# A linear-attention and Fourier-mixing kernel whose first part's order of steps is written anew

## The chip, the cores and the metric

The kernel runs on one core of a Trainium2 chip. A core has TensorE (PE) for matrix products, VectorE (DVE), ScalarE (ACT) and GpSimd (POOL) for the rest, SyncE (SP), from whose queue nearly all DMAs are issued here, and 16 DMA engines that move data between the device's memory (HBM) and the on-chip buffer (SBUF). TensorE writes only to PSUM, which has eight banks. The metric is the device time of one launch in microseconds (us): the median of several runs. A profile is one more execution, recorded instruction by instruction.

## The reference, cut to what matters

The inputs are q, k, v of shape (8 batches, 8 heads, 576 rows, 64), omega (128 x 64), and two weights, 512 x 2048 and 2048 x 512, given in double precision. In outline:

```python
def phi(x):                              # x is q or k, scaled by 64 ** -0.25
    h = x @ omega.T - sum(x * x) / 2
    return exp(h - max(h)) / sqrt(128)
kv  = phi(k).T @ v;  z = sum(phi(k))     # per batch and head
att = phi(q) @ kv / (phi(q) @ z + 1e-6)
x   = att, heads side by side            # (8, 576, 512)
u   = x + real(fft2(x))                  # over rows and columns of each batch
un  = (u - mean(u)) / sqrt(var(u) + 1e-6)
out = u + relu(un @ w_ch1) @ w_ch2
```

## The kernel before

**Two parts.** The program has a first part, which does attention, the Fourier mixing, the narrowing of the weights from 64 to 32 bits and the first 512 of the 4608 rows of the MLP, and a second part, which does the other 4096 rows in eight blocks of 512 with a scheme of seven products for eight. The second part is the larger, and the change leaves its instructions and their order alone. It begins on TensorE with the first product at line 1359.

**Streams.** The first part is written as generators, called streams, which yield a `Step` (line 103) ahead of each piece of work: the engines that may do it, what it needs to be finished, which buffers and PSUM banks it takes and gives back. The streams, in the order in which they are handed to `listing.run` (line 1319): `first` (omega transposed), `loads` (line 391: k and q of two heads, 288 KB each, into two buffers called `kq`), `loads_v` (line 411: v of two heads, three buffers `vd`), `load_tables` (line 441), `frames`, `plain_norms`, `mixing` (line 766 for each batch), three times `pairs` (each takes every third pair of heads through `attn`), `w2_parts`, `weight_sums`, `block_norms`, `plain` (line 1112: the MLP of the first rows), `weights` (line 480: 32 loads of 512 KB into four buffers `slab`, each followed by `narrow`) and `warm`. A stream can fork others, such as an eviction from PSUM that may wait while the stream goes on.

**One pair of heads** (`attn`, line 611) is: wait for k and q; transpose them by 64-wide matmuls against an identity (line 525) and copy them out (564 on DVE, 566 on ACT); 72 small products with omega (line 644); row maxima on DVE (587); exponentials on ACT (604); 72 small products with v (678); another transpose; products with kv (725 and 733); the division (742 to 754). The mixing of a batch folds its rows and columns by symmetries on DVE and POOL (782 to 823), multiplies with cosine and sine tables on TensorE (844, 854, 894), adds the halves up (943 to 961) and stores the result in HBM (930, 975, 986). `plain` is 512 products of 128 columns (1143) and 128 products of 512 columns (1166). They need nothing of the pairs of heads that are then in work, only rows mixed before and narrowed weights.

**What sets the order.** Each engine runs its instructions in the order in which the program lists them. That order is not found while the program is built: the string `PICKS` (line 65) holds it. `Listing.run` (line 204) keeps a list `todo` of the streams that have a step to do. For each step it reads two characters. The first is a place in `todo`; the second holds, as 9 times the choice of engine plus the PSUM bank, which engine of those that the step allows does the work and in which bank its product goes (8 stands for none; so "h", which is 17, is the second engine with no bank):

```python
pick = next(picks, None)
n = place(pick) if pick else 0
other, self.bank = divmod(place(next(picks)), 9) if pick else (None, None)
...
for item in todo if pick is None else [todo[n]]:
    got = self.start(*item[2:], other=other)
```

A stream whose step is done goes to the end of `todo`. `Listing` also keeps a model of time with the constants of `FIRST` (line 51) and the costs of the steps. Where `PICKS` is read it decides nothing but what it records; it is with such a replay that a string like `PICKS` is searched. As `FIRST` and the steps stand in the kernel, the model knows the loads' time on the DMA engines (270 bytes per ns, one after the other), but nothing of TensorE's instructions having to be fetched.

The instructions of all engines are in HBM, and are brought in while the program runs. The profile lists these transfers as queues of the kind "instruction".

Of the kernel before, what the change touches and what calls it, by code (L numbers as in the profile page):

```python
# [39 lines left out]
class Clock(NamedTuple):  # L40
# [22 lines left out]


PICKS = (
    "4818f8d0f808e3e8d848d4d8d6e20838b8c4f6e8g8a8f8a8f8f8b4ehb8e8e8d4e0dhd8b2d8f8a838e478a8a6bhdh92d8e888b4dhc8b6d8"
    "b4e890ehe2e898h8ghb8j808a4i8i87880i878h488j8ahi8i8g8b8c8h0h88876h2g8i8f0h8e8h8e8g8g8c6fha8e4fh88c0i6i8j8g8i8g8"
    "j8j8g4i8d2j8j898j8a6j8h8dhj8j8f8f8j8i8e0i8f6ih78d2hhbhh8g0hhc8g4g8f8e6h2g8d4i0a8d898h8f898i8c6chj8k8c4j8b8j8h0"
    "i8i8j8j8a6i8i898i8f4i8i818ah78c2i6i8ahb8i4j0i86898dhb8k8k85898k6l4k8k8a2khb8j6i4l0l8i868d8d858g6e2i8f8e8m8m8i8"
    "chn0k8o868h8n8n8ihn8n8n8g4mhl2m8c8m8j8m8k498n868n8h6e2m858d8d6f898i8i878b860e4i6h8h898h8b8c2g88858h8b6i4a8j8j8"  # L70
    "d8b8h8e8i8ghb2h89878b8ch68d8j860l6l8l2d8n8k8j8l8l888i864ghi8b8i8d8j8j888g876j0i8ihg8h4khk6k8i8bhf8k8j8j87078k8"
    "68g898k8j8j8d4k8k886khk0kh68g86hj8j8g8a8h878i6i8g288l8i4d0p6g8m2n8b8l8k88878b8a8h8a6k8j8f0k8k87878h8h8d4j8k8j6"
    "e8fhe0g8k8i8e8j8h2k8l8k4k8j8g8k89h68i8e8d2lh68d0m2m8lh98n8a6e8q8q8q8h8c8m8m0o8n898a8o8b6n8f8b2m8l8m888m8m8g808"
    "h8k87894n098f8l8e6l8j868d8f858b85892g0d6i4f8j8e8g848h8i8jhihg8e8i858a0h8h8b4a8g8e8i8d898i8c8i0i8h8h2i8c0c842jh"
    "b8j8i6h2j8f8gh58i8e0khk4kh48j6k8i8d0m8c2g8n888hhk6n8j8d8e4n8n8a8n8i8i0m8g8h89hm898e8b8c6c8j864i8f88hc8h8j8i8k8"
    "32k3l5khj878j0l1i8ghc8l848f8l8d8i8l6e868l8m8l8i8a8i2n8h8chj8l8l878k874l0m2n6khk858j858l4l8l0f8k898e2b8ehh878a8"
    "i8d858d6h4g8g8d8i898j888hh60khk1l2m3khi8nhb878b8hhb8m898eh96khk2k8k4khb8a8j8i0j8i8h882j6j8k8i8j8j8e8h4h8i8i888"
    "f868f8d0f8f8f858f8f85658f85248f0g8ehc8f8f848b8c1e3d8d8d0dh74d86872dh7hdha0f84876i4h8h8d0i258g848i8f8e6i4g8h8d8"
    "h870k2j8e8k8k8i8j8j8c4i8i8d0i8g6j8e8g4k882k8987hi8i8b8g4kh88k86898d853k2e8m8i8iha8f838k878l8i8c8k84448i848b8g2"
    "h8f858h8h8d8g8a84460k6j8j8h8j888j8j8a2i8i0j8k8k866chk864f8m89858n848kh8880ohj8d2o8h6o8g8m0o2p6n8o868q868j8f8b8"  # L80
    "n8c8n8n8m8d8m8d8o8nhh8h8q8e8a8n8d8n8j8g8d0n2nhk8n8g8h866m8m858l8e8e8fhg878m8c858c0k2k8a878k8b8j856k898k8e888c8"
    "80h298i8i8d8i888a8f8c8d0d8c8f8g8d8f8f8d6f2f8d8c8e8g87858e8a8f86808dhd8dhdha8a8c5e2e846f0g2eh88g8b8c8ch98c82834"
    "c8c8c896c8c852c8c0d4c8d6d8cha0ch88c8c8b298d4dhd6dhb868a0b8c8b2c8d848chc8b4c856e7dhe0dhdh82e688a8e878dhd8d8dh80"
    "dh4898d89488d8d890ch98c898c8c86hb8b8d878d8d8d866d8d7e2f3d8f0f8ehd864e0f266chchd4f8c880e8a2f3989hf8f8f8f868d4f8"
    "dh80fh67f868eh9864c8c87856b8b83880b8b888b4c608bh68c8c8c8c89hb8b852b8483038c2d6d83874e5dh8880e638987hb818834h6h"
    "f8f8f868a8e8f898g8d8chhhh8h8a8a8h8c86660i8i8a8j8e8b8i8i854fhi0j838f8e8f8jhjhe838a8l8l898m8m8m8i8m8b6l8b8k4l8k8"
    "f068m888i8a8h868e8i8j4h8j8j8j8j876k0j8ihkh68h8h6l2l8g8f5h8a8i8m8ihg8k8h4j8j0j8j2ehj5l6g8i8l8g8k8k878k8h8g8g7fh"
    "9892ihf8h4i0d8j8h8gh26i2h860j8g8i8c5h868589hhh50g84hg84888e8a2f3a8g898a0b8b8ah68f8e8e8b8d8dh18b2d8e866f4d898h8"
    "h8dhc8h88842h8a41830i8i8i8f85h7h42hhh5hh6he8h8e8g8g8g8g8gh8890g2g8fh96f89894f890fh98f89hc692f8e4dh68e082g8e8g8"
    "c8f838c6f882g890g8g8b8a2f8687h94g0b898a8g8e6f8h2dhchd8f4f85hdhb0eh46e8g888c4gh90g877ghe0c8g4j6i8k898d3k2l848c8"  # L90
    "l8l8e8k8k8485hih50j6c8j4h8k8k898h8g8j8d8i8f0i8ehf858h896h0ghfhhhh8h8h8h8h8e4i6e8g8h0h8e418i8i8b8f8c8g818a8d8ah"
    "08d8h890b8h4f8h8386876h8f86848a8h828h8h8hhhhd8983h38h8h88876h8a8g4h0g8g8d85888g8f8f80812f8d8c8dh445860f8e88228"
    "b8g886g81888f0f8f4a8g89hdh96eh78d8f8c8b0e432f82878b8e8a8d86888d868d856d8a852d888a6d8e8e8ehc898e8b4e850f8f6ghg2"
    "g8f8g8e8f8ah66gh5872g8e4g886g8b8d2f8a8c0g4g8a878g876b872c8f8a8e4b8g8g8a2h858i8c8c4h8h868g8a8h8c0g8c8g8f4fh76f8"
    "68c0f868a858d86hd868c882ch9476d8d0d878b2c89698a4b8b8b0a888986888a8a8b6c4b8886298b8a8a85898989h8698a8a848448888"
    "42885h8h48609h5894a09h82b6b8948hb08846b8c898b852a878a8869858ah88a850a8a88h88528478468898886844567h70825854965h"
    "5h6888886898429h90989498929888a89ha84098987488467898989898989h6828a8a0a8a1b2c3chc4d5e0589hd1f3g74hehf3b8b8b8f8"
    "fhg8f8089846d878883885489h5h81a6a8884h9834960818a8289828308248380824766855988878989h98a85888888888567h086h4818"
    "98685878686818384858083848083848282838182818081808"
)  # L100


# [1578 lines left out]
```

## Time and profile before

| | |
|---|---|
| time, median of 3 runs | 1172.77 us (1171.44 to 1174.62) |
| the profiled execution | 1177.47 us, of which span 1175.7 |
| granted TensorE clock, mean | 0.992 |
| instruction transfers, q8 | 103 packets, 1.69 MB |
| instruction transfers, q14 | 48 packets, 0.39 MB |
| all other transfers | 218.35 MB |
| TensorE's first product of the second part | at 425 us |

The span is the time from the first to the last instruction of the profiled execution; the rest of its time lies around it. "Busy" is the time in which an engine ran at least one instruction. In lists of instructions the first two numbers are start and duration, and what stands in brackets is the idle time ahead of the instruction and what ended it. A DMA share is the mean busy share of the 16 DMA engines. A loaded stationary operand (PEld) and a matmul are an instruction each.

### The profile page before, as it was taken

The page shows a single profiled execution, that of the slowest core. Times are in us where ns is not written, and L with a number is a line of the kernel's source. Part 1 is how long each engine was busy: PE and PEld are TensorE (multiplying, and loading weights), DVE is VectorE, ACT ScalarE, POOL GpSimd, SP SyncE. Part 2 cuts the span into 40 slices and gives each one's busy share as a digit, 9 for nine tenths or more (in the row PEclk, how much of TensorE's full clock was granted, in tenths as well). Part 3 has the DMA queues.
Part 4 walks back from the last instruction along what each step waited for, and adds up shares of the span by engine and source line. Part 5 has one row for each costly group of instructions (what it writes and reads, how often), then busy time and mean ns, then how long its engine had stood idle before and what let it go on. Part 6 is the DMA issues. An engine that isn't in the chain of part 4 may idle for free.

```text
span 1175.7 us, 32543 instructions
## 1 busy us (share of the span) xinstructions
PE 1139.7 (97%) x13045; PEld 1019.1 (87%) x13045; DVE 745.3 (63%) x1562; ACT 433.8 (37%) x1426; POOL 441.3 (38%) x509
## 2 busy tenths in 40 slices
PE   8878899999999999999999999999999999999998
PEld 7767886869777968998998998998999899899898
DVE  6888788777687674744754664574573574474255
ACT  6888786436678212122112212212212212211211
POOL 2463464337243326225225324414513502522421
PEclk9999999999999999999999999999999999999999
DMA  7776747556653263872783693593495396388156
GB/s 239 204 245 183 230 155 231 191 159 222 203 154 92 69 181 110 264 264 82 228 274 112 178 307 97 156 319 123 126 322 170 91 278 233 81 248 270 38 167 202
DMA packets 167223, 220.43 MB, mean 187 GB/s; under 512 B 50080, under 2 KB 81056, under 8 KB 167072
## 3 DMA queue, kind: packets, MB, share of 16 engines
q1 hardware_dynamic: 166576, 218.09, 60.2%
q8 instruction: 103, 1.69, 0.6%
q14 instruction: 48, 0.39, 0.1%
q10 hardware_dynamic: 496, 0.26, 0.1%
HBM read 179.24 MB, written 43.25 MB: 189 GB/s over the span
## 4 chain that ended last, share of the span: by engine, by line
PE 84%; DVE 5%; ACT 4%; DMA 3%; issue 2%; SPq 1%; POOL 0%; DVEq 0%; POOLq 0%; ACTq 0%
PE banks L1359 33%; PE banks L1539 27%; PE banks L1143 5%; PE banks L644 4%; PE banks L1166 4%; DMA wl<-w2l 3%; PE banks L525 3%; ACT e L604 3%; PE banks L678 2%; PE banks L725 2%; DVE nmx L587 1%; PE banks L844 1%; PE banks L894 1%; PE banks L854 1%; DVE w L474 1%
## 5 line engine op out<-in xcount | busy, mean ns | idle before, releaser
L1539 PE MATMUL banks<-wl,sums 128*128 128x128 f32 x1792 | 218.8, 276 | 0.0
L1539 PEld LDWEIGHTS banks<-wl,sums 128*128 128x128 f32 x1792 | 210.0, 193 | 0.1
L1345 DVE CUSTOM_DVE_ANT_0 hid<-banks,s 128x256 f32<-128x256 f32 x192 | 81.1, 424 | 190.9 <-PE banks L1359 190.5
L604 ACT ACTIVATE e<-banks,nmx 128x128 f32<-128x128 f32 x576 | 157.2, 414 | 39.8 <-DVE nmx L587 39.0
L1373 ACT ACTIVATE s<-banks 128x256 f32<-128x256 f32 x192 | 73.6, 383 | 253.8 <-PE banks L1359 253.8
L1359 PE MATMUL banks<-unT,w 128*128 128x256 f32 x704 | 166.3, 379 | 0.0
L1359 PEld LDWEIGHTS banks<-unT,w 128*128 128x128 f32 x704 | 133.2, 190 | 18.3 <-issue 0.5
L1579 POOL TENSOR_TENSOR ur<-ur,part 128x512 f32<-128x512 f32 x32 | 46.9, 1465 | 270.0 <-ACT part L1572 195.7
L1514 ACT ACTIVATE s<-banks 128x128 f32<-128x128 f32 x168 | 46.6, 277 | 258.3 <-PE banks L1539 223.8
L1359 PE MATMUL banks<-tt,w1s 128*128 128x256 f32 x512 | 126.2, 379 | 0.0
L1359 PEld LDWEIGHTS banks<-tt,w1s 128*128 128x128 f32 x512 | 97.1, 190 | 13.5
L1539 PE MATMUL banks<-wl,hid 128*128 128x128 f32 x768 | 100.6, 277 | 4.3 <-DMA wl<-w2l 4.0
L587 DVE TENSOR_REDUCE nmx<-banks 128x8 f32<-128x1024 f32 (+1 forms) x96 | 88.4, 950 | 25.7 <-PE banks L644 25.3
L1519 DVE TENSOR_TENSOR part<-banks,s 128x128 f32<-128x128 f32 x168 | 48.9, 291 | 86.5 <-PE banks L1539 85.4
L1539 PEld LDWEIGHTS banks<-wl,hid 128*128 128x128 f32 x768 | 94.4, 192 | 7.5 <-DMA wl<-w2l 6.0
L644 PE MATMUL banks<-om,kqT 64*64 64x128 f32 (+1 forms) x2088 | 83.1, 283 | 8.0 <-issue 3.5
L644 PEld LDWEIGHTS banks<-om,kqT 64*64 64x64 f32 (+1 forms) x2088 | 69.1, 145 | 18.4 <-issue 5.6
L1359 PE MATMUL banks<-unT,w1s 128*128 128x256 f32 x320 | 79.5, 379 | 0.0
L1539 PE MATMUL banks<-wl,hs 128*128 128x128 f32 x576 | 75.0, 275 | 0.4 <-DVE part L1519 0.4
L1426 POOL TENSOR_TENSOR hs<-hid,hs 128x256 f32<-128x256 f32 x64 | 50.0, 782 | 57.3 <-issue 37.2
L1539 PEld LDWEIGHTS banks<-wl,hs 128*128 128x128 f32 x576 | 70.1, 192 | 0.9 <-DVE part L1519 0.6
L478 POOL TENSOR_TENSOR w<-w,raw 128x512 uint32<-128x512 uint32 x32 | 43.6, 1370 | 69.7 <-ACT raw L461 30.0
(133 smaller groups left out, 1870.6 us busy)
## 6 DMA issues: line engine op xcount, KB each, us to landing
wl<-w2l SPq DMA_DIRECT2D x392, 256.0 KB
raw<-in_moe_w_ch_dram SPq DMA_DIRECT2D x32, 512.0 KB
kq<-in_k_dram SPq DMA_DIRECT2D x32, 288.0 KB
kq<-in_q_dram SPq DMA_DIRECT2D x32, 288.0 KB
vd<-in_v_dram SPq DMA_DIRECT2D x32, 288.0 KB
u<-us SPq DMA_DIRECT2D x36, 256.0 KB
ur<-us SPq DMA_DIRECT2D x36, 256.0 KB
out_dram<-ur SPq DMA_DIRECT2D x34, 256.0 KB
```

The source lines that it names most:

```text
L587: nc.vector.tensor_reduce(nmx[:, :, 0:num], pps[:, :, 0 : MF * num].rearrange("p b (c m) -> p b c m", m=MF), axis=AX.X, op=ALU.max, negate ...
L604: nc.scalar.activation(out=e[:, c + (i if num == 1 else 0), :], in_=pps[:, i, MF * c : MF * c + MF], func=AF.Exp, bias=nmx[:, i, c : c + 1],)
L644: nc.tensor.matmul(pps[cols, c, MF * m : MF * m + MF], lhsT=kqT[rows, j, cols], rhs=om2[rows, :],)
L1143: nc.tensor.matmul(hp[:, 0:TP], lhsT=w1[:, dc, 128 * fc : 128 * fc + 128], rhs=unTs[key][:, dc, :], start=(dc == 0), stop=(dc == NDC - 1),)
L1166: nc.tensor.matmul(yp[:, 0:DM], lhsT=hs[fc][:, 128 * i : 128 * i + 128], rhs=w2[:, fc, :], start=(fc == 0), stop=(fc == NFC - 1),)
L1345: nc.vector._custom_dve(TENSOR_ADD_SAT, out=o, in0=ps, in1=sb, s0=FMAX, s1=0.0)
L1359: nc.tensor.matmul(ps[:, 0:HT].rearrange("f (b q) -> f b q", q=Q), lhsT=left(dc), rhs=right(dc), start=start and dc == 0, stop=(dc == D2 - 1),
L1373: nc.scalar.activation(out=s[:], in_=ps[:, 0:HT], func=AF.Copy)
L1426: nc.gpsimd.tensor_tensor(out=o, in0=l, in1=r, op=op)
L1519: nc.vector.tensor_tensor(out=part[:, t, 128 * m : 128 * m + 128], in0=ps[:, 0:128], in1=saved[with_][:], op=ALU.add,)
L1539: nc.tensor.matmul(ps[:, 0:128], lhsT=left[:, f], rhs=wls[j, i, n][:, f], start=start and f == 0, stop=(f == 3), skip_group_check=True,)
L1579: eng.tensor_tensor(out=o, in0=o, in1=other, op=ALU.add)
```

## The change

The string `PICKS` is replaced by another of the same length, 3680 characters for 1840 steps. Nothing else is touched: neither the streams, their steps and costs, nor the constants, nor the second part. The new string comes from a search with a replay that counts, beside the loads, the transfers of TensorE's instructions, which are placed behind the loads. This replay is not in the kernel.

What the string holds can differ in the order of the steps of all engines and of SP's DMAs, in the engine where a step allows two, and in the banks. The count of "second engine, no bank" is 185 in the old string and 175 in the new one.

```diff
 PICKS = (
-    "4818f8d0f808e3e8d848d4d8d6e20838b8c4f6e8g8a8f8a8f8f8b4ehb8e8e8d4e0dhd8b2d8f8a838e478a8a6bhdh92d8e888b4dhc8b6d8"
...
-    "98685878686818384858083848083848282838182818081808"
+    "18f8f8e0f808e3e858d4e6d8e2d8d8e808b8b4e8f8e648f0fhf0g418c8a8chc89898f808b882f878d8d0eha8d6ehe2e828e0f6ehc8dh98"
...
+    "5878467888488868281h484858484848280818282828081808"
 )
```

Read by hand, the start of the new string says: the load of the first k (18; place 1 is the stream `loads`), of the first q (f8, where that stream has gone to the end of the list) and of the second k (f8), then the warm-up products in bank 0 (e0), the transpose of omega in bank 3 (e3) and its scaling (e8), the first pair's transposes (d4, e6) and its first product (e2). The old string has the same steps there, with the second k behind the transpose of omega.

## The prediction

> **What bounds the kernel now.** First the table of busy times and the shares of the chain that ended last, on the page of the profile, then two windows that part the span where the second half's first product (L1359) starts, 425 us:
>
> ```profile
> PE 1139.7 (97%) x13045; PEld 1019.1 (87%) x13045; DVE 745.3 (63%) x1562; ACT 433.8 (37%) x1426; POOL 441.3 (38%) x509
> PE 84%; DVE 5%; ACT 4%; DMA 3%; issue 2%; SPq 1%; POOL 0%; DVEq 0%; POOLq 0%; ACTq 0%
> ...
> 0.00:425.00 425.00, 397.82 (x8118) 326.50 (x8119) 330.20 (x739) 279.25 (x947) 185.45 (x193) 0.98 0.60 183
> 425.00:1175.70 750.70, 741.91 (x4929) 692.55 (x4927) 415.14 (x823) 154.60 (x479) 255.84 (x316) 1.00 0.61 190
> ```
>
> The columns of the windows are length, then busy time and count of PE, weight loads, DVE, ACT and POOL, granted clock, DMA share, GB/s. TensorE is the bound throughout. The change can only touch the first 425 us, where TensorE idles 425.0 - 397.8 = 27.2 us. The order of steps alone changes, so the 397.8 us stay, except where the clock was low; the question is what becomes of 27.2 us.
>
> Next, the timeline of TensorE for the idle time of its matmuls, with what ended it. "issue" means that the instruction waited for nothing that the profile shows:
>
> ```profile
> 22.04 0.39 PE L678 MATMUL banks<-vd,e 64*64 64x65 f32 x10 [1.62 <-issue]
> 44.49 0.56 PE L678 MATMUL banks<-vd,e 64*64 64x65 f32 x19 [2.48 <-issue]
> 73.99 0.28 PE L725 MATMUL banks<-kv,qeT 128*64 128x65 f32 x2 [1.41 <-issue]
> 89.09 1.40 PE L678 MATMUL banks<-vd,e 64*64 64x65 f32 x61 [1.66 <-ACT e L604]
> 91.45 2.65 PE L678 MATMUL banks<-vd,e 64*64 64x65 f32 x83 [0.96 <-issue]
> 139.17 0.66 PE L644 MATMUL banks<-om,kqT 64*64 64x128 f32 x5 [2.34 <-issue]
> 207.31 0.44 PE L525 MATMUL banks<-ident,kq 64*128 64x64 f32 x5 [1.44 <-issue]
> 207.68 3.76 PE L644 MATMUL banks<-om,kqT 64*64 64x128 f32 x72
> ...
> 303.31 2.20 PE L644 MATMUL banks<-om,kqT 64*64 64x128 f32 x72
> ```
>
> With 1.14 at 85.25, 0.84 at 299.17 and 0.31 at 358.78, nine such gaps make 12.54 us, nearly half of the idle time. They stop in the middle of a run of like matmuls. Windows laid from one gap to the next say why:
>
> ```profile
> 73.50:84.90 11.40, 8.16 (x254) 6.95 (x255) 9.37 (x19) 9.03 (x26) 5.76 (x5) 1.00 0.92 279
> 84.90:91.20 6.30, 3.58 (x128) 3.13 (x127) 4.94 (x10) 4.70 (x18) 2.65 (x2) 1.00 0.72 229
> 91.20:138.00 46.80, 42.85 (x1016) 37.86 (x1017) 41.29 (x97) 40.32 (x128) 23.29 (x22) 0.96 0.68 211
> 138.00:207.00 69.00, 64.93 (x1270) 50.37 (x1269) 56.86 (x116) 48.68 (x154) 37.50 (x31) 0.98 0.65 198
> ```
>
> Between gaps lie 254, 128, 1016 and 1270 matmuls: 2, 1, 8 and 10 times 127, each with its weight load. So TensorE's instructions come in blocks of some 254. The queue table of the first 425 us has 64 transfers of kind "instruction" on q8, 1.05 MB, some 16 KB each, and 8118 / 127 = 64. The gaps sit on borders of blocks; nine of 64 borders stall. Which ones, windows of 10 us show by the DMA share:
>
> ```profile
> 40.00:50.00 10.00, 7.35 (x242) 6.42 (x240) 7.11 (x16) 7.51 (x24) 6.66 (x8) 1.00 0.93 257
> 50.00:60.00 10.00, 9.52 (x212) 8.13 (x206) 9.47 (x20) 9.74 (x35) 0.59 (x1) 1.00 0.52 140
> 130.00:140.00 10.00, 7.66 (x191) 6.78 (x192) 5.96 (x13) 8.50 (x31) 5.73 (x4) 0.96 1.03 309
> 200.00:210.00 10.00, 8.56 (x257) 8.02 (x257) 6.53 (x16) 2.36 (x7) 3.58 (x2) 0.88 1.00 334
> ```
>
> All gaps fall where the share is 0.87 or more (for the one at 90.49, the burst ends at 89.9), and none where it is near the mean of 0.60. A block asked for during a burst of loads arrives late.
>
> **The change part by part.** It replaces the 1840 picks of the first part: which stream's step is next, on which engine, in which bank. Every instruction stays.
>
> *Gaps for instructions.* 12.5 us now. Bounds: none left (-12.5), or bursts met at more borders (nine gaps of mean 1.4 us, so three more are +4). The bursts come from SP's queue order: at 128.6 to 141 it issues raw weights, k, the returned half, v, q, raw and v back to back, while 370 to 400 runs at shares of 0.01 to 0.06. Raw weights (32 of 512 KB) and the order of v against k can be moved; the borders are known for each order, every 127 matmuls, so a replay that counts them can keep bursts off. I take three or four of nine left, 5 us: -7.5. That is nearer to none left, as the windows near a share of 0.6 show no gap.
>
> *The clock behind a gap.* Rows behind long idle time run slow: the 72 matmuls at 207.68 take 3.76 us against 2.20 at 303.31 (+1.56). So estimated, 83 of L678 at 91.45 cost 2.65 against 1.47 (72 take 1.28 at 148.23), +1.2; the products from 139.76 to 143.57 3.81 against 2.48 from 200.15 to 202.63, +1.3; twenty wide ones at 23.11 2.36 against 1.38 (36 take 2.48 at 26.79), with the transposes behind them +1.2. In sum 5.3 us, bounds -5.3 and, with two more, +2.8. Removed in proportion to the gaps: -3.0. [...]
>
> *What is late next.* The other idle time, 27.2 - 12.5 = 14.7 us, is the start (1.0), waits for ACT (L604 3.1), DVE and short pieces. In unstalled stretches ACT and DVE are almost full: 9.74 and 9.47 of 10 us at 50:60, where TensorE still idles 0.48. Time that TensorE wins in the attention stretches is partly handed to them: 0.5 to 0.9 us per 10 us, over the some 50 us around bursts, 2.5 to 4.5. Also, a later load delays what waits for it: no matmul of the first part waits for a load now, but POOL waits 22.5 us for raw weights (L467). I take +3.5; bounds 0 (the cover holds: loads are early, and the plain MLP's products at L1143 and L1166, 121 us of matmuls, fill TensorE) and +11 (rival 2).
>
> *The queues.* SP's first five loads stay k, q, k, v, q, read by hand from the string; then v of the second pair goes ahead of the third k. That k needs a free buffer (it issues at 5.76, behind the transposes), so the first microseconds are worth 0, with v filling a queue that would be idle; if v delays k by its 288 KB, at 265 GB/s it is 1.1 us once, inside the +3.5. Engine choices change little by count (185 second choices become 175), so the loads on DVE, ACT and POOL stay near 330, 279 and 185 us: 0. POOL's instructions move with the conversions that feed w1 and w2; its 185 of 425 us are the cover. The 425 us border: the last 35 us there are plain products with TensorE full, and the second half needs the sums made before; if these came late the wait would stand at the first L1359; 0, as POOL and DVE have 240 and 95 us free.
>
> Sum: -7.5 - 3.0 + 3.5 = -7.0 us. Against the profiled execution's 1177.5 us (span 1175.7 and 1.8 around it) that is 1170.5; that execution lies 4.7 above the median of the runs, 1172.8, from which the prediction is 1165.8.
>
> **The rivals.**
> 1. *The gaps only move.* A replay that is off by a fraction of a block, or takes a wrong delay for a transfer, clears the nine borders and meets a burst at as many others. The same comes out if a block is slowed by whatever traffic there is and not by the queue of loads ahead of it. For it: bursts last 5 to 15 us, several blocks of small matmuls long (127 of L678 take 2.2 us). Against: the borders lie so regularly, and no gap stands in windows near 0.6. Time: -2 to +2, so 1172.8.
>    [...]
> 2. *The fillers go to the wrong place (slower).* To keep borders out of bursts, slow plain products are put beside the loads, as a block of L1143 lasts 127 x 0.118 = 15 us against 2.2 us of L678; they are then missing between the attention steps, where ACT and DVE set the pace. For it: ACT waits 39.0 us for the row maxima (L587) even now. Price: idle 0.9 instead of 0.5 us per 10 us over 375 us, +15, against -10.5: 1177. From 0.28 us per 10 us on it outweighs the gain.
> 3. *All of it goes.* The gaps and the clock loss vanish, and the waits grow by 2 alone: -17.8 + 2 = -15.8, so 1157.
>
> **How the numbers follow.** 0.3% is 3.5 us, about what a measurement of this kernel can tell from no change. The forecast (-4 to -13) has 0.48, rival 3 0.10, rival 1 0.18, rival 2 0.24. Rival 1 is nearly all within 0.3%; a search fits its replay, not the chip, so rival 2, whose waits the replay only estimates, keeps its weight. Faster 0.58, same 0.18, slower 0.24. The range takes in rival 1 and the middle of rival 2, and reaches down close to rival 3: 1157 to 1181; the forecast's own is 1160 to 1169.
>
> **What would show it.** TensorE's busy time in the first part near 395 us, its end near 418; issue gaps of matmuls 4 to 6 us in all; shares over 0.87 in fewer than the eight windows of 10 us; waits for ACT and DVE up by some 3 us. The second part's 750.7 us within 1 us. If the gaps stay at 12 us, or ACT and DVE waits of TensorE rise by over 10, the prediction is wrong.

## The result, and the profile after

The new order takes 1167.22 us (median of 20 runs, 1161.9 to 1172.5) against 1175.21 us for the old one in the same comparison (20 runs, 1170.4 to 1182.72). The ratio is 0.9926, 95% interval 0.9907 to 0.9944: by the ratio some 8.7 us faster, by the medians 8.0. The prediction was -7.0 us.

The page of the new order has these busy times and this chain:

```profile
PE 1137.0 (97%) x13045; PEld 1014.9 (87%) x13045; DVE 750.5 (64%) x1579; ACT 437.7 (38%) x1426; POOL 423.8 (36%) x492
PE 86%; DVE 5%; DMA 4%; ACT 3%; issue 1%; SPq 0%; POOL 0%; DVEq 0%; ACTq 0%; POOLq 0%
```

The part of the chain called "issue" went from 2% to 1%. Two windows part the new execution at the first product of the second part; the columns are those of before:

```profile
0.00:414.11 414.11, 395.13 (x8117) 322.24 (x8118) 335.46 (x756) 282.86 (x947) 167.20 (x176) 1.00 0.61 185
414.11:1166.50 752.39, 741.82 (x4929) 692.65 (x4927) 414.99 (x823) 154.88 (x479) 256.61 (x316) 1.00 0.62 191
```

The first part ends at 414.1 instead of 425.0 us, 10.9 us earlier. The second part, where no instruction was moved, takes 752.4 instead of 750.7 us, 1.7 us more; that will need an explanation of its own. The granted clock of the first part went from 0.98 to 1.00.

In TensorE's timeline of the first part, these are all the gaps with nothing to wait for, and the two longest waits for data:

```profile
39.16 0.97 PE L725 MATMUL banks<-kv,qeT 128*64 128x65 f32 x25 [1.04 <-issue]
81.14 2.12 PE L644 MATMUL banks<-om,kqT 64*64 64x128 f32 x61 [1.55 <-ACT e L604]
102.20 0.57 PE L678 MATMUL banks<-vd,e 64*64 64x65 f32 x22 [0.20 <-issue]
135.74 2.15 PE L1143 MATMUL banks<-unT,w 128*128 128x128 f32 x16 [0.60 <-issue]
198.61 1.32 PE L644 MATMUL banks<-om,kqT 64*64 64x128 f32 x40 [2.02 <-DVE kqT L564]
208.11 0.60 PE L1143 MATMUL banks<-unT,w 128*128 128x128 f32 x4 [0.34 <-issue]
```

Gaps for instructions are 2.18 us in sum, where they were 12.54; the other listed gaps are 15.0 us, where they were 13.5. TensorE is busy 395.1 instead of 397.8 us for the same products, at a granted clock of 1.00 instead of 0.98. So -10.4, +1.5 and -2.7 give -11.6, near the measured -10.9; the rest is in gaps too short for the timeline to list.

One of the four gaps for instructions is of another kind. Counted in matmuls, the gaps at 39.16, 102.20 and 208.11 lie on borders of blocks, as all nine of the old order do. The one at 135.74, before products at L1143, lies some 20 matmuls ahead of a border. It comes at this same product, with 0.59 to 0.62 us, in every other execution of the new order below but the one with more loads, also where the borders are shifted and where the loads are thinned. So it is no late block. What it waits for was not found. In the tables below it is counted with the gaps for instructions.

The bursts of loads did not vanish. Windows of 10 us with a DMA share of 0.87 or more were eight, and are five:

```profile
20.00:30.00 10.00, 9.13 (x259) 7.93 (x259) 9.07 (x20) 10.00 (x35) 3.73 (x3) 1.00 0.90 274
160.00:170.00 10.00, 9.82 (x114) 6.04 (x113) 9.79 (x22) 7.23 (x20) 6.93 (x6) 1.00 0.93 296
180.00:190.00 10.00, 9.43 (x216) 6.30 (x212) 7.10 (x11) 7.96 (x28) 5.08 (x5) 1.00 0.95 271
240.00:250.00 10.00, 10.00 (x156) 5.97 (x153) 9.03 (x16) 4.68 (x17) 2.23 (x3) 1.00 0.89 257
300.00:310.00 10.00, 10.00 (x176) 5.81 (x168) 5.95 (x14) 7.43 (x28) 1.10 (x2) 1.00 0.91 299
```

None of these five windows has a gap for instructions; those that are left on borders lie in windows with a share of 0.64 to 0.85. The number of such windows is not what sets the two orders apart: in the executions below with the loads as they are it is five to eight under the new order and six to eight under the old one. What changed beside it is the count of matmuls in them: in four of five it is 114 to 216, a block of 127 every 6 to 11 us. Before, the eight windows had 157 to 274 matmuls, mean 226.

The blocks can be counted in all these executions. Take those that have a DMA share of 0.87 or more in the 4 us behind their border: under the old order they are 18 to 25 of 62 (three executions), under the new one 17 to 23 (eight executions). Of these, 9 to 12 are used up in less than 5 us under the old order, gaps not counted, and 2 to 6 under the new one.

### When a block is asked for

Two counts of the traces show how a block comes. The border of a block is every 127 matmuls; the moment of its transfer is where the count of packets on q8 goes up in windows that end a quarter of a microsecond later each. Side by side, times in us, where the last column but one is where the next block begins (worked out from these counts, to some 0.3 us):

| order | a block begins | transfer of the next | after | next block begins | from the transfer | gap |
|---|---|---|---|---|---|---|
| old | 79.45 | 83.00 | 3.6 | 85.3 | 2.3 | 1.14 |
| old | 85.34 | 89.00 | 3.7 | 91.4 | 2.4 | 0.96 |
| old | 133.20 | 137.00 | 3.8 | 139.3 | 2.3 | 2.34 |
| old | 202.44 | 205.00 | 2.6 | 207.5 | 2.5 | 1.44 |
| old | 109.47 | 110.75 | 1.3 | 114.6 | 3.8 | none |
| new | 203.57 | 206.00 | 2.4 | 208.2 | 2.2 | 0.34 |
| new | 125.60 | 126.25 | 0.7 | 130.9 | 4.6 | none |

In these rows the next block's transfer comes 0.7 to 1.3 us behind the border where TensorE did not wait, and 2.4 to 3.8 us behind it where it did; its instructions then ran 2.2 to 2.5 us after the transfer. Over all blocks of the two executions the mean from border to transfer is 2.6 (old) and 1.9 us (new) where the DMA share in the 4 us behind the border is 0.87 or more, and 0.8 and 0.9 us where it is under 0.6. The single values spread widely, from 0.3 to 4.9 us in bursts, so a burst does not delay every block alike; and in a few blocks the transfer comes up to 1.7 us ahead of the border. At all the gaps on borders, in all executions of this document, the instructions ran 2.2 to 3.2 us after the transfer. So in these traces one block was brought in ahead, not more. A gap comes where a block is used up in less than the two together, which by these means is an estimate of some 3 us in quiet and 4 to 5 us in a burst. In these two executions it came at nine borders of the old order and at three of the new one.

### The profile page after: what moved, and what is told of

Same layout as the page of the kernel before. It is cut to its first block, busy times and chain, and to the rows that moved or that the text cites. A ratio compares the mean times of both kernels' runs of the same rounds, so it can differ in the third digit from the quotient of the medians.

```text
span 1166.5 us, 32529 instructions
## 1 busy us (share of the span) xinstructions
PE 1137.0 (97%) x13045; PEld 1014.9 (87%) x13045; DVE 750.5 (64%) x1579; ACT 437.7 (38%) x1426; POOL 423.8 (36%) x492
## 4 chain that ended last, share of the span: by engine, by line
PE 86%; DVE 5%; DMA 4%; ACT 3%; issue 1%; SPq 0%; POOL 0%; DVEq 0%; ACTq 0%; POOLq 0%
PE banks L1359 33%; PE banks L1539 27%; PE banks L644 5%; PE banks L1143 5%; PE banks L1166 4%; DMA wl<-w2l 3%; PE banks L525 3%; PE banks L725 2%; PE banks L678 2%; ACT e L604 2%; PE banks L844 1%; PE banks L894 1%; DVE nmx L587 1%; PE banks L854 1%; DVE x L754 1%
## 5 line engine op out<-in xcount | busy, mean ns | idle before, releaser
L1539 PE MATMUL banks<-wl,sums 128*128 128x128 f32 x1792 | 218.7, 276 | 0.0
L1539 PEld LDWEIGHTS banks<-wl,sums 128*128 128x128 f32 x1792 | 210.0, 193 | 0.0
L1539 PE MATMUL banks<-wl,hid 128*128 128x128 f32 x768 | 100.5, 277 | 6.1 <-DMA wl<-w2l 5.9
L1539 PEld LDWEIGHTS banks<-wl,hid 128*128 128x128 f32 x768 | 94.3, 192 | 9.3 <-DMA wl<-w2l 7.8
L644 PE MATMUL banks<-om,kqT 64*64 64x128 f32 (+1 forms) x2088 | 80.0, 278 | 5.5 <-DVE kqT L564 2.0
L644 PEld LDWEIGHTS banks<-om,kqT 64*64 64x64 f32 (+1 forms) x2088 | 66.0, 141 | 15.2 <-DVE kqT L564 2.3
L1539 PE MATMUL banks<-wl,hs 128*128 128x128 f32 x576 | 75.0, 275 | 0.4 <-DVE part L1519 0.4
L1539 PEld LDWEIGHTS banks<-wl,hs 128*128 128x128 f32 x576 | 70.1, 192 | 0.9 <-DVE part L1519 0.6
L1359 PEld LDWEIGHTS banks<-unT,w1s 128*128 128x128 f32 x320 | 60.4, 190 | 8.7
```

The lines of the kernel that those rows point to most:

```text
L644: nc.tensor.matmul(pps[cols, c, MF * m : MF * m + MF], lhsT=kqT[rows, j, cols], rhs=om2[rows, :],)
L1359: nc.tensor.matmul(ps[:, 0:HT].rearrange("f (b q) -> f b q", q=Q), lhsT=left(dc), rhs=right(dc), start=start and dc == 0, stop=(dc == D2 - 1),
L1539: nc.tensor.matmul(ps[:, 0:128], lhsT=left[:, f], rhs=wls[j, i, n][:, f], start=start and f == 0, stop=(f == 3), skip_group_check=True,)
```

## The experiments

### Shifting the borders

If the new order wins by exact places of the borders (theory F), moving all borders by a part of a block must bring the gaps back. If it wins by something else in the order (O), nothing happens. The warm-up at the very start, six products (12 matmuls), was replaced by 22, 38 or 54 tiny ones, which move the borders by a quarter, a half and three quarters of a block. Only the 22 move hardly anything else: the warm-up takes 2.5 us with them, 4.2 with 38 and 5.9 with 54, where it was 2.9, so that the first pair's transposes begin 0.1, 1.2 and 2.9 us later than in the new order as it is:

```diff
-        for _ in range(6):
-            nc.tensor.matmul(ps[:, 0:128], lhsT=ur1[:, 0:128], rhs=ur1[:, 0:128])
+        for _ in range(22):      # 38, 54
+            nc.tensor.matmul(ps[0:32, 0:1], lhsT=ur1[:, 0:32], rhs=ur1[:, 0:1])
```

> The new order, with the six warm-up products (24 instructions on TensorE) replaced by 22 tiny ones (88), about as long in sum: every block border of TensorE's instructions moves by 64 instructions, a quarter of a block, and nothing else. Theory F (the gain is that borders are kept clear of bursts of loads): borders now fall where the search did not put them; issue gaps of matmuls in the first part rise from 2.2 us to 4 to 10 us, clock rows under 1.00 come back at the longer ones, the first part ends 3 to 12 us later than 414.1, time 1169 to 1179. Rival O (the gain is another merit of the order, fewer waits for data): gaps stay under 3 us, end within 1.5 us of 414.1, time within 2 us of the new order's.

> [...] F: issue gaps 4 to 12 us, time 1169 to 1180, the worst of the shifts or near it. O: gaps under 3 us, time within 2 us of the new order's.

> [...] F: issue gaps 4 to 10 us, time 1170 to 1180. O: gaps under 3 us, time 0 to 2 us above the new order's.

> The old order with 38 tiny warm-up products, borders moved by half a block. F: the old order was not fitted to its borders, so gaps are dealt anew: the nine places change, the sum is 5 to 15 us, still at multiples of some 127 matmuls from one to the next, time 1168 to 1182. O: the gaps stay where they are, since they belong to the loads and not to the count of instructions; time within 2 us of the old order's.

| order, shift | gaps for instructions, us | first part ends | time, median | ratio to the old order, interval |
|---|---|---|---|---|
| new, a quarter | 2.63 | 412.9 | 1164.87 | 0.9870 (0.9842 to 0.9899) |
| new, half | 2.98 | 416.8 | 1166.24 | 0.9879 (0.9854 to 0.9905) |
| new, three quarters | 6.46 | 420.5 | 1171.22 | 0.9946 (0.9920 to 0.9973) |
| old, half | 11.31 | 424.5 | 1174.51 | 0.9952 (0.9928 to 0.9975) |

Theory F missed for a quarter and a half: the gaps stay under 3 us. It came true for three quarters, with 6.5 us, and for the old order, where the gaps were dealt anew with 11.3 us in sum. O was right on the gaps for a quarter and a half, but it missed as well: the gaps of the old order did move with the borders. (Of the later ends of the first part, 1.2 us for a half and 2.9 us for three quarters are the longer warm-up.) The old order's timeline with half a block of shift has its longest ones here:

```profile
47.80 0.90 PE L525 MATMUL banks<-ident,e 64*128 64x64 f32 x11 [3.00 <-issue]
93.19 0.56 PE L678 MATMUL banks<-vd,e 64*64 64x65 f32 x19 [2.11 <-issue]
143.54 0.57 PE L725 MATMUL banks<-kv,qeT 128*64 128x65 f32 x13 [1.47 <-issue]
205.59 0.45 PE L678 MATMUL banks<-vd,e 64*64 64x65 f32 x13 [1.38 <-issue]
```

They lie at other instructions than before, but again where many loads are about: the windows of 10 us that they end in have DMA shares of 1.07, 0.92, 0.95 and 0.79. Hence theory G, by the table above: what counts is how fast blocks are used up while a burst lasts; the exact border decides only which of the fast blocks pays. One thing in this table G does not explain: by its ratio the new order is faster with a quarter or half a block of shift than without (0.9926), and so is the old one. It comes back below.

### Fewer and more loads

G says that the same instructions in the same order should run without most gaps if the loads are thinned, and that the new order should lose its lead then; and that more traffic brings the gaps back. The raw weights are 16.8 MB of the first part's loads and can be thinned by themselves. A quarter of each is loaded, and the narrowing reads that quarter four times over:

```diff
-        lo, hi = raw[:, :, 0], raw[:, :, 1]
+        lo = raw[:, :, 0]
+        hi = raw[:, 0 : CV // 4, 1].unsqueeze(1).to_broadcast([P, 4, CV // 4])
...
-                nc.sync.dma_start(raw[:].rearrange("p n two -> p (n two)"), src.bitcast(U32))
+                part = slice(0, CV // 2)
+                nc.sync.dma_start(raw[:].rearrange("p n two -> p (n two)")[:, part], src.bitcast(U32)[:, part])
```

and for more traffic a copy from memory to memory follows each raw load:

```diff
                 nc.sync.dma_start(raw[:].rearrange("p n two -> p (n two)"), src.bitcast(U32))
+                more = dram.tile([128, 2 * CV], U32, name=f"more{i}")
+                nc.sync.dma_start(more[:, :], src.bitcast(U32))
```

> The old order, unchanged, with a quarter of each raw weight loaded (128 KB of 512) and the narrowing reading that quarter four times over in steps of the same size, so that 12.6 MB of the first part's loads are gone and the engines' work stays; what is left out is the other three quarters of the weights' values. Theory G, formed after the shifts: a block is asked for when the one before it begins; its transfer starts 0.2 to 1.4 us later with few loads about and 2.5 to 3.8 us later in a burst, and 2.3 us behind that it can be used, so that a gap comes where a block is used up faster than that, whatever the exact border. G expects the gaps behind bursts of raw weights (20, 43, 73, 84, 90, 137 us, 9.95 us in sum) to shrink to some 2 us, those at 207 and 299, behind other transfers, to stay: issue gaps 4 to 6 us, clock back at 1.00 in most rows, time 8 to 14 us under the old order's, near the new order's. Rival O (the new order has fewer waits for data): the old order's other idle time of 13.5 us stays and so does the time, within 3 us; gaps 10 to 13 us.

> The new order with the same quarter loads. G: little is left to win, issue gaps 2.2 to under 1.5 us, time 0 to 3 us under the new order's, and within 4 us of the old order with the same loads. O: as far from the old order with the same loads as the new order is from the old one, 8 to 9 us.

> The new order with one more transfer of 512 KB, from memory to memory, behind each raw weight's load (16.8 MB in the first part), of which nothing is used. G: the bursts last longer, issue gaps come back to 6 to 14 us with clock rows under 1.00, time 8 to 20 us above the new order's, most of it in issue gaps. Rival L (what counts is only that data are late): waits for data grow, with POOL and SP waiting longer for raw weights and k and q, issue gaps stay under 4 us.

| order, loads | gaps for instructions, us | other listed gaps | first part ends | time, median | ratio, interval |
|---|---|---|---|---|---|
| old, thin | 5.52 | 15.3 | 413.4 | 1166.91 | 0.9893 (0.9837 to 0.9949) |
| new, thin | 1.33 | 15.9 | 413.4 | 1165.85 | 0.9892 (0.9838 to 0.9946) |
| new, thick | 11.13 | 18.5 | 433.2 | 1182.59 | 1.0029 (0.9998 to 1.0060) |

The windows of the first parts, old order with thin loads first, then new order with thin loads:

```profile
0.00:413.35 413.35, 391.32 (x8118) 320.72 (x8118) 331.62 (x739) 278.12 (x947) 185.37 (x193) 1.00 0.54 158
```

```profile
0.00:413.35 413.35, 394.13 (x8118) 321.54 (x8118) 336.66 (x756) 282.21 (x947) 167.43 (x176) 1.00 0.53 155
```

With thin loads both orders end their first part at the same time and run equally long, to within intervals of half a percent. The old order gains 11.6 us in its first part from this alone: 7.0 in gaps for instructions and 6.5 in busy time, with its clock back at 1.00, less 1.8 in other gaps and 0.1 in short ones. The new one gains 0.8 us against its first execution and 4.5 against its second one, shown below. The equal ends are a sum of two unequal parts: the new order still has 4.2 us less in gaps for instructions, and the old one is busy for 2.8 us less. The order as such is not better at waiting for data (15.3 against 15.9 us). Its lead exists only where the loads are there, which speaks for G and against O.

G's sum of 4 to 6 us came out, but not its parts. The gaps at the bursts with raw weights were to shrink from 9.95 to some 2 us; 4.2 are left (1.07, 1.20, 1.74 and, at a border that had no gap before, 0.22 us). Of the two behind other transfers, which were to stay, the first has 1.12 us, at 198, and the one near 299 is gone.

With more traffic the gaps come back under the new order, among them these, and the clock of its first part falls to 0.98:

```profile
23.00 0.35 PE L680 MATMUL banks<-vd,e 64*64 64x65 f32 x8 [1.83 <-issue]
115.83 0.62 PE L680 MATMUL banks<-vd,e 64*64 64x65 f32 x22 [1.73 <-issue]
148.12 0.87 PE L646 MATMUL banks<-om,kqT 64*64 64x128 f32 x19 [1.68 <-issue]
```

This profiled execution is the slowest of its ten, 5.5 us above their median. Its first part ends 19.1 us later than in the first execution of the new order: +9.0 in gaps for instructions, +7.3 in busy time (at the granted clock of 0.98), +3.5 in waits for data. So late data (rival L) is a smaller part.

### The new order again, and what the shift had done

The quarter shift had looked faster than the new order itself. Both were run on one chip, with a third kernel whose warm-up is six tiny products, as many instructions as the original has, so that nothing shifts.

> The new order as it is, for a comparison on one chip with the two that follow: 0.991 to 0.994 of the old order's time, as before.

> The new order with 22 tiny warm-up products once more, beside the new order on the same chip. Theory S (the quarter shift of the borders and the shorter warm-up give a real gain: the first part ended 1.3 us earlier, 36 products at L644 behind the first transposes took 3.40 us instead of 4.21): 1 to 2 us under the new order. Theory N (its lead of 5 us in the first look was mostly the second part's waits for w2l blocks, 1.8 against 5.9 us, which change from run to run): 0 to 2 us under, within the interval.

> The new order with six tiny warm-up products: as many instructions as before, so that the borders stay, but a warm-up of some 0.5 us. S, borders: no gain of the 1.3 us, the first part ends at 414 or later; if the early end comes from the warm-up, it ends as with 22 tiny ones, near 413. [...]

| new order | gaps for instructions | first part ends | second part takes | waits for w2l in it | time, median | ratio, interval |
|---|---|---|---|---|---|---|
| as it is | 2.62 | 417.8 | 754.2 | 8.2 | 1170.08 | 0.9927 (0.9903 to 0.9952) |
| a quarter shifted | 2.60 | 417.9 | 746.3 | 1.9 | 1165.28 | 0.9891 (0.9857 to 0.9925) |
| six tiny products | 3.11 | 417.0 | 750.5 | 6.2 | 1170.52 | 0.9919 (0.9891 to 0.9947) |

Theory S (the shift or the shorter warm-up is a gain of the first part) missed its reason: the first parts end within 0.9 us of each other. N (the second part's waits change by chance) missed too: the difference is in the second part, but both executions of the quarter shift have short waits (1.8 and 1.9 us) and both of the order as it is have long ones (5.9 and 8.2). The groups of TensorE's waits in the new order as it is begin with this line, the products at L1539 waiting for blocks of w2 (tile wl):

```profile
PE banks L1539 <- DMA wl<-w2l: 8.2, 6, 2.3
```

Over all executions profiled up to here, the wait is 4.0 to 8.2 us in the seven whose borders were not shifted and 0.6 to 2.5 us in the five that were, with either order. The second part starts between 413.4 and 433.2 us in the seven and between 412.9 and 424.5 us in the five, so when it starts does not decide this. In the first execution of the new order the timeline shows one of the waits:

```profile
931.44 4.63 PE L1539 MATMUL banks<-wl,sums 128*128 128x128 f32 x40
938.11 1.54 PE L1539 MATMUL banks<-wl,hid 128*128 128x128 f32 x8 [2.04 <-DMA wl<-w2l]
```

A block of TensorE's instructions is transferred at 934.5, 1.6 us before this wait begins. The same holds for other long waits: transfers at 840.0 and 1029.5 before waits that begin at 842.2 and 1032.1, and in the second execution 937.25 and 1033.0 before 940.6 and 1035.3. In the quarter-shifted kernel's first execution the transfers near this place are at 924.0 and 942.75, and the wait that ends at 933.24 is 0.55 us. Over all executions of this document, 17 such waits are of 1.2 us or more; each begins 1.8 to 3.8 us behind the start of a block's transfer.

So a last edit moves the borders by a quarter of a block only behind the first part, with 16 tiny products ahead of the second part's first product:

```diff
         xb, x = got()
+        for _ in range(16 if (j, fc) == (0, 0) else 0):
+            nc.tensor.matmul(x[0:32, 0:1], lhsT=ident[:, 0:32], rhs=ident[:, 0:1])
         product(x, lambda d: w1[:, d, f], lambda d: un[0][:, :, d], True)
```

> The new order, with 16 tiny products (64 instructions on TensorE, some 1.8 us) ahead of the second part's first product: borders stay as they are in the first part and move by a quarter of a block in the second. Theory T (the 4 to 8 us that the second part waits for blocks of w2 come from a block of TensorE's instructions being fetched 1.5 to 3.5 us ahead of them, and a shift by a quarter takes it out of that place): waits for w2l under 3 us in the second part, the first part as it was, time 2 to 5 us under the new order's, ratio 0.988 to 0.991. Rival U (these waits depend on the warm-up or on when the second part starts): 4 to 8 us as before, time 1 to 2 us above the new order's.

> The old order with the same 16 tiny products. T: waits for w2l from 4.0 to under 2.5 us; the first part's issue gaps stay at some 12 us and in their places; time 0 to 3 us under the old order's. U: waits of 3 to 6 us, time 1 to 2 us above the old order's.

TensorE's waits for these blocks, from the groups of waits of the new order with the late shift, and then of the old order with it:

```profile
PE banks L1541 <- DMA wl<-w2l: 1.7, 4, 0.7
```

```profile
PE banks L1541 <- DMA wl<-w2l: 2.1, 4, 1.1
```

The old order's first part is what it was, with 12.3 us of gaps for instructions and an end at 423.8; the new order's has 4.7 us of gaps in this execution and ends at 417.2, both with 1.2 us of tiny products in it. The new order with the late shift has a median of 1164.08 us, ratio 0.9884 (0.9850 to 0.9919); its second part takes 746.2 us. The old order has 1176.25 us, ratio 0.9982 (0.9953 to 1.0012), which the interval does not part from no change. Theory T holds in the profile, for both orders: waits under 3 us, and a second part that is some 6 to 8 us shorter with the new order and 4.0 with the old one. Waits are not all of it: of the 6.2 us against the new order's first execution 4.2 are waits for these blocks and 1.9 are busy time. In time the new order with the late shift stands 0.4% below the new order as it is (0.9884 against 0.9926 and 0.9927), though the intervals overlap. The lowest ratios with full loads are those of the quarter shift (0.9870 and 0.9891), the half shift (0.9879) and this one; by its interval only the first of them (0.9842 to 0.9899) is clear of both measurements of the new order as it is.

Why loads of wl come late some microseconds behind a block's transfer was not tested. A transfer is one packet and takes 1.1 us (0.6% of 16 engines' 1175.7 us, for 103 packets).

## Why the prediction was right, and where not

*The gaps for instructions, -7.5.* Measured -10.4 in the first pair of executions. Over four unshifted executions of the new order in its first part (2.2, 2.6, 3.1, 4.7 us) against two of the old (12.5, 12.3) it is -7.6 to -10.4. Of this, 0.6 us in each execution of the new order is the gap that is no late block, so the late blocks lost a little more. The step was right, its size at the low end. Its reason was only half right. It said that a replay can keep bursts off the known borders; the shifts by a quarter and a half, with gaps of 2.6 and 3.0 us, show that the exact borders matter little, while three quarters brought 6.5 us back. What the new order has is fewer fast blocks during bursts (2 to 6 instead of 9 to 12); it does not have fewer bursts in all its executions. The prediction's sign for it, fewer windows of 10 us with a share over 0.87, came in the first execution (five) and not in the second (eight), where the gaps were nearly as short (2.6 against 2.2 us). With thin loads the old order's gaps fell from 12.5 to 5.5 us, and with more loads the new order's rose from 2.2 to 11.1 us: the loads are the cause.

*The clock, -3.0.* Measured -2.7 in busy time, with the granted clock at 1.00 in every window of 10 us of the first part. The number is right by luck. Even in the old order not every gap cost clock: the windows of 10 us with those at 22.04, 91.45, 139.17 and 207.31 have a granted clock of 0.83 to 0.96, but behind the longest, 2.48 us at 44.49, the windows from 40 to 60 us have 1.00. The prediction put the whole loss at 5.3 us and let a part of it go; the whole loss went, and busy time fell by half of the 5.3. The old order with thin loads, also at 1.00, is busy for 6.5 us less than before. So it seems that the new order spends some 3 us more of busy time for another reason; which one stays open.

*Waits for data, +3.5.* Measured +1.5 in the first execution and +4.7 in the second (18.2 against 13.5). Right within its bounds. In the first execution waits for DVE rose from 5.7 to 9.6 us and waits for ACT fell from 7.8 to 4.8; no matmul waits there for a load.

*The queues, 0.* The sixth load is v, ahead of the third k, as read by hand; the start of the first pair's work is within 0.1 us of before (4.30 and 4.38 us for the first transposes). POOL is busy 18 us less in the first part, with 17 instructions less, and DVE 5 us more, with 17 more. Whether the longer waits for DVE come from that was not tested.

*The second part, within 1 us.* This was wrong. It grew by 1.7 us in the first execution and by 3.5 in the second, by the waits for w2l. The prediction took the second part for closed, since no instruction of it is moved. Its waits depend on where a block border falls beside the loads of wl: with the late shift they were 1.7 us under the new order, where they had been 5.9 and 8.2. That how those two meet changes with the first part was not shown. Why it was 2 to 4 us worse under the new order and not better was not settled; other executions with unshifted borders had 5.4 to 6.5 us.

*The sum.* The forecast was -7.0; the result is -9.2 between the two profiled executions and -8.7 by the ratio. Part of the closeness is luck: gaps that fell by up to 2.9 us more than forecast stand against a second part that took 1.7 to 3.5 us more. The first part's end was forecast near 418 us and came at 414.1 and 417.8.

*The rivals.* Rival 1, that the gaps only move, did not come: they fell to a fifth, in the worst execution to two fifths. Its ground, that a block is slowed by whatever traffic there is, is not refuted; thinning the loads thins that traffic. Rival 2, fillers in the wrong place, did not come either: the other listed gaps grew by 1.5 to 4.7 us, not 15, although slow blocks do stand beside the bursts now. Rival 3, that all goes, is near for the gaps, -10.4 of -12.5, and for the clock rows; in time, -8.7 against -15.8, it is not.

## What to carry to other kernels

Where TensorE runs small matmuls and idles with nothing to wait for, count the instructions between the gaps: in the old order here they were multiples of 127 matmuls, and the gaps, 12.5 us in sum, were blocks of instructions that arrived late. The gap that stayed at the same instruction when idle instructions were put ahead (0.6 us before products at L1143) was something else. The cure here was loads in bulk beside slow matmuls and fast matmuls beside few loads: 2 to 6 instead of 9 to 12 of the blocks in bursts were used up in less than 5 us, and the gaps of the first part were 2.2 to 4.7 us. That held without an exact fit to the borders for shifts of a quarter and a half of a block (2.6 and 3.0 us), and less so for three quarters (6.5 us). Where a load is just in time, look whether a block's transfer starts shortly before it is waited for (1.8 to 3.8 us before the waits here); 64 idle instructions, placed ahead, moved it out of the way here, and the waits went from 5.9 and 8.2 us to 1.7.

## What the runs showed of the hardware that was not expected

In these traces a block of some 254 instructions is transferred at about the time at which the one before it begins: on the mean 0.8 to 0.9 us behind that where few loads are about and 1.9 to 2.6 us behind it in a burst. Where TensorE had to wait for it, it ran 2.2 to 3.2 us behind the start of its transfer. A block of nothing but products with v (L678) would be used up in some 2.2 us (72 take 1.28), so by this estimate it would wait even in quiet; no run has one.

16 tiny products at the head of the second part, 1.2 us of work, took 2 to 6.5 us of waits out of the 750 us behind them. They moved the transfers of instructions; the long ones of the waits that went had begun 1.8 to 3.4 us behind such transfers.
